# A squeeze-and-excitation gate on one core: 21-row chunks with finer read and write pieces, a shorter gate chain, and the weights on another queue

## Chip, cores, metric

The kernel runs on 1 core of one Trainium2 chip. The metric is the device time of one execution in microseconds (us). The kernel before takes 308.88 us, median of 5 runs (308.16 to 309.18). Single profiled executions have a "span", from first to last instruction, which is about 1.8 us shorter than the time of the run.

## The reference

```python
# x: (1, 256, 256, 384) bf16, w_down: (384, 24), w_up: (24, 384)
def reference(x, w_down, w_up):
    s = x.mean(axis=(1, 2))
    s = _sigmoid(_silu(s @ w_down) @ w_up)
    return x * s[:, None, None, :]
```

All of x must be read before the first output is known. x is 65,536 rows of 384 bf16 values, 50.33 MB. On the core it is laid out as 128 partitions with 512 rows each; below, "a row" is one such row on all 128 partitions, 98,304 bytes. The kernel before keeps 272 of the 512 rows on chip from the first reading to the write (17 slots of 16), so the other 240 are read a second time.

## The kernel before

It has two phases. In the read phase, chunks of 16 rows are loaded into 17 slots in rotation, and TensorE sums the rows by a matmul with ones. Then a short chain on several engines turns the sum into the gate `s_bc`. In the write phase, the 17 chunks still in the slots (272 rows) are multiplied by the gate on VectorE and written; each slot that has been written is filled again with one of the 15 chunks (240 rows) that were overwritten, which is then multiplied and written too.

```python
R = max(1, min(RPP, (16 * 1024) // (C * 2)))   # 21 ...
while R > 1 and RPP % R != 0: R -= 1           # ... cut down to 16, a divisor of 512
S_fit = max(1, (avail - 256) // slot_bytes)    # 17 slots
...
# the last chunk is read as 14 + 2 rows, every other one whole
# write pieces: slot 0 as 2,4,10 rows, slot 1 as 8,8, the others whole
...
# TensorE, per row:   ps_S[0:32, 0:384] += ones^T @ row
# gate chain:
for k in range(NK):                            # VectorE: three scalings into partitions 0, 32, 64
    v.tensor_scalar(out=mean3[32*k:32*k+1, 0:P], in0=ps_S[0:1, k*P:(k+1)*P], scalar1=inv_count, ...)
pe.matmul(ps_mT[:, 0:NK], mean3[0:65, 0:P], sel[0:65, 0:NK])   # transpose by a 65-row matmul
v.tensor_copy(meanT, ps_mT)                    # then w_down, silu, w_up, sigmoid -> s_bc
...
for it in items:                               # write phase, VectorE
    for (lo, hi) in it["pieces"]:
        v.tensor_tensor(slots[s][:, lo:hi, :], slots[s][:, lo:hi, :], s_bc..., ALU.mult)
        # the scalar queue then writes this piece; the sync queue refills the slot when all its pieces are out
```

Of the kernel before, what the change touches and what calls it, by code (L numbers as in the profile page):

```python
# [4 lines left out]



def bass_standalone__se_block__vision_kernel(
# [4 lines left out]
    out: bass.AP,  # L13
    rows_per_chunk=None,
    max_slots=None,
):
    dt = mybir.dt
    ACTF = mybir.ActivationFunctionType
    ALU = mybir.AluOpType
    bf16 = dt.bfloat16  # L20
    f32 = dt.float32

    P = nc.NUM_PARTITIONS
    B, H, W, C = x.shape
    Cw, RED = w_down.shape
# [4 lines left out]
    RPP = NROWS // P  # L30
    assert C % P == 0 and C <= 512
    NK = C // P
    assert NK <= 4
    assert RED <= P
    inv_count = 1.0 / float(NROWS)

    if rows_per_chunk is None:
        R = max(1, min(RPP, (16 * 1024) // (C * 2)))
        while R > 1 and RPP % R != 0:
            R -= 1  # L40
    else:
        R = max(1, min(int(rows_per_chunk), RPP))
    chunks = []
    rs = 0
    while rs < RPP:
        nr = min(R, RPP - rs)
        chunks.append((rs, nr))
        rs += nr
    NCH = len(chunks)

    xr = x.flatten_outer_dims().rearrange("(p n) c -> p n c", p=P)
# [4 lines left out]
    with contextlib.ExitStack() as es:  # L56
        E = es.enter_context

        ones = E(nc.sbuf_tensor("se_ones", [P, M1], bf16))
        s_bc = E(nc.sbuf_tensor("se_sbc", [P, C], bf16))  # L60
        mean3 = E(nc.sbuf_tensor("se_mean3", [P, P], bf16))
        sel = E(nc.sbuf_tensor("se_sel", [P, NK], bf16))
        meanT = E(nc.sbuf_tensor("se_meanT", [P, NK], bf16))
        wd_sb = E(nc.sbuf_tensor("se_wd", [P, NK, RED], bf16))
        wu_sb = E(nc.sbuf_tensor("se_wu", [P, C], bf16))
# [1 line left out]
        dT = E(nc.sbuf_tensor("se_dT", [P, P], bf16))  # L67

        ps_S = E(nc.psum_tensor("se_psS", [P, C], f32))
        ps_mT = E(nc.psum_tensor("se_psmT", [P, NK], f32))  # L70
        ps_d = E(nc.psum_tensor("se_psd", [P, 1], f32))
        ps_u = E(nc.psum_tensor("se_psu", [P, C], f32))

        slot_bytes = R * C * 2
        avail = nc.sbuf_bytes_remaining
        S_fit = max(1, (avail - 256) // slot_bytes)
        S = min(NCH, S_fit)
        if max_slots is not None:
            S = max(1, min(S, int(max_slots)))
        assert S >= 2 or NCH == 1  # L80
        slots = [E(nc.sbuf_tensor(f"se_slot{i}", [P, R, C], bf16)) for i in range(S)]

        sem_rd = [E(nc.semaphore(f"se_rd{i}")) for i in range(S)]
        sem_wr = [E(nc.semaphore(f"se_wr{i}")) for i in range(S)]
# [1 line left out]
        sem_dve = E(nc.semaphore("se_dve"))  # L86
        sem_w = E(nc.semaphore("se_w"))
        sem_ones = E(nc.semaphore("se_onesm"))
        sem_z = E(nc.semaphore("se_z"))
        sem_init = E(nc.semaphore("se_init"))  # L90
        sem_mean3 = E(nc.semaphore("se_m3"))
        sem_mT = E(nc.semaphore("se_mT"))
        sem_meanT = E(nc.semaphore("se_meanT"))
        sem_d = E(nc.semaphore("se_d"))
# [1 line left out]
        sem_dT = E(nc.semaphore("se_dTs"))  # L96
        sem_u = E(nc.semaphore("se_u"))
        sem_sbc = E(nc.semaphore("se_sbcs"))
        sem_tail = E(nc.semaphore("se_tail"))

        slot_of_chunk = [t % S for t in range(NCH)]
        NB = NCH - S
# [3 lines left out]
        for t in range(NCH):  # L106
            s = slot_of_chunk[t]
            fill_cnt[s] += 1
            phase1_fill_idx.append(fill_cnt[s])
        p1_pieces = []  # L110
        for t in range(NCH):
            rs_, nr = chunks[t]
            s = slot_of_chunk[t]
            if t == NCH - 1 and nr > 2:
                cut = nr - 2
                p1_pieces.append([(0, cut, sem_rd[s], 16 * phase1_fill_idx[t]), (cut, nr, sem_tail, 16)])
            else:
                p1_pieces.append([(0, nr, sem_rd[s], 16 * phase1_fill_idx[t])])

        items = []  # L120
        for s in range(S):
            c = resident_chunk_of_slot[s]
            nr = chunks[c][1]
            if s == 0:
                cuts = [0, min(2, nr), min(6, nr), nr]
            elif s == 1:
                cuts = [0, min(8, nr), nr]
            else:
                cuts = [0, nr]
            cuts = sorted(set(cuts))  # L130
            pieces = [(cuts[i], cuts[i + 1]) for i in range(len(cuts) - 1)]
            items.append(dict(chunk=c, slot=s, stream=False, pieces=pieces, fill_idx=phase1_fill_idx[c]))
        wr_cnt = [0] * S
        fill_cnt2 = list(fill_cnt)
# [12 lines left out]
        assert sorted(it["chunk"] for it in items) == list(range(NCH))  # L147

        with nc.Block() as block:
            @block.gpsimd  # L150
            def _(g):
                g.dma_start(wd_sb[:, :, :], w_down.rearrange("(k p) r -> p k r", p=P)).then_inc(sem_w, 16)  # L152
                g.dma_start(wu_sb[0:RED, :], w_up[:, :]).then_inc(sem_w, 16)  # L153

            @block.sync
            def _(sp):
                for t in range(NCH):
# [16 lines left out]
            @block.vector  # L174
            def _(v):
                v.memset(ones[:, :], 1.0).then_inc(sem_ones, 1)  # L176
                v.memset(mean3[:, :], 0.0).then_inc(sem_z, 1)  # L177
                v.memset(sel[:, :], 0.0).then_inc(sem_z, 1)
                v.wait_ge(sem_z, 2)
                for k in range(NK):  # L180
                    v.memset(sel[32 * k:32 * k + 1, k:k + 1], 1.0).then_inc(sem_init, 1)  # L181
                v.wait_ge(sem_pe, NCH)
                v.wait_ge(sem_z, 2)
                for k in range(NK):
                    v.tensor_scalar(  # L185
                        out=mean3[32 * k:32 * k + 1, 0:P],
                        in0=ps_S[0:1, k * P:(k + 1) * P],
                        scalar1=inv_count,
                        scalar2=None,
                        op0=ALU.mult,  # L190
                    ).then_inc(sem_mean3, 1)
                v.wait_ge(sem_mT, 1)
                v.tensor_copy(meanT[:, 0:NK], ps_mT[:, 0:NK]).then_inc(sem_meanT, 1)  # L193
                v.wait_ge(sem_sig, 1)
                v.wait_ge(sem_d, 1)
                v.tensor_tensor(  # L196
                    dT[0:RED, 0:P],
                    ps_d[0:RED, 0:1].broadcast_to([RED, P]),
                    sig[0:RED, 0:1].broadcast_to([RED, P]),
                    ALU.mult,  # L200
                ).then_inc(sem_dT, 1)
                v.wait_ge(sem_sbc, 1)
                for it in items:
                    s = it["slot"]
                    first = True
                    for (lo, hi) in it["pieces"]:
                        if first:
                            v.wait_ge(sem_rd[s], 16 * it["fill_idx"])
                            first = False
                        v.tensor_tensor(  # L210
                            slots[s][:, lo:hi, :],
                            slots[s][:, lo:hi, :],
                            s_bc[:, None, :].broadcast_to([P, hi - lo, C]),
                            ALU.mult,
                        ).then_inc(sem_dve, 1)

            @block.tensor
            def _(pe):
                pe.wait_ge(sem_ones, 1)
                n_mm_total = sum(nr for _, nr in chunks)  # L220
                mm_i = [0]

                def row_mms(s, lo, hi):
                    ins_ = None
                    for r in range(lo, hi):
                        ins_ = pe.matmul(  # L226
                            ps_S[0:M1, 0:C],
                            ones[:, 0:M1],
                            slots[s][:, r, :],
                            start=(mm_i[0] == 0),  # L230
                            stop=(mm_i[0] == n_mm_total - 1),
                        )
                        mm_i[0] += 1
                    return ins_

                for t in range(NCH):
                    s = slot_of_chunk[t]
                    ins = None
                    for (lo, hi, sm, wv) in p1_pieces[t]:
                        pe.wait_ge(sm, wv)  # L240
                        ins = row_mms(s, lo, hi)
                    ins.then_inc(sem_pe, 1)
                pe.wait_ge(sem_mean3, NK)
                pe.wait_ge(sem_init, NK)
                pe.matmul(ps_mT[:, 0:NK], mean3[0:32 * (NK - 1) + 1, 0:P], sel[0:32 * (NK - 1) + 1, 0:NK]).then_inc(sem_mT, 1)  # L245
                pe.wait_ge(sem_meanT, 1)
                pe.wait_ge(sem_w, 32)
                ins = None
                for k in range(NK):
                    ins = pe.matmul(  # L250
                        ps_d[0:RED, 0:1],
                        wd_sb[:, k, 0:RED],
                        meanT[:, k:k + 1],
                        start=(k == 0),
                        stop=(k == NK - 1),
                    )
                ins.then_inc(sem_d, 1)
                pe.wait_ge(sem_dT, 1)
                pe.matmul(ps_u[:, 0:C], dT[0:RED, 0:P], wu_sb[0:RED, 0:C]).then_inc(sem_u, 1)  # L259

            @block.scalar
            def _(act):
                act.wait_ge(sem_ones, 1)
                act.activation(sig[32:33, 0:1], ones[32:33, 0:1], ACTF.Sigmoid)  # L264
                act.wait_ge(sem_d, 1)
# [40 lines left out]
```

## Time and profile before

| reading | value |
|---|---|
| span of the profiled run | 306.7 us |
| last row matmul over, chain begins (chain of waits) | 125.4 us |
| `s_bc` ready | 128.5 us |
| from `s_bc` to the end | 178.2 us |
| a chunk of 16 rows in the read phase (timeline) | 3.69 us |

The page of the kernel before, first its slices (DMA is the mean busy share of the 16 DMA engines in tenths, GB/s what they moved in each fortieth of the span), then the bytes.

```profile
DMA  7999999999999997089999999999999999999998
GB/s 287 429 420 430 421 426 429 420 428 426 423 428 423 426 429 329 16 318 383 428 426 429 429 425 423 428 434 433 423 428 436 434 425 425 434 434 426 428 429 346
HBM read 73.96 MB, written 50.33 MB: 405 GB/s over the span
```

DMA is at work in nearly all slices, at 420 to 436 GB/s outside the start, the dent and the end. That the rate itself has little left is an estimate from these slices: none is above 436, and one at 428 is usual. So two ways to gain stand out: move fewer bytes, or shrink the dent in slices 16 to 19, where the read phase ends and the writes begin.

The timeline of the kernel before in that dent (columns: start us, duration us, engine, line, operation, output and inputs, count, and in brackets the idle time before it with its releaser).

```profile
119.30 2.77 PE L226 MATMUL se_psS<-se_slot,se_ones 128*32 128x384 bf16 x16 [0.91 <-DMA se_slot<-in_x_dram]
122.65 2.77 PE L226 MATMUL se_psS<-se_slot,se_ones 128*32 128x384 bf16 x16 [0.58 <-DMA se_slot<-in_x_dram]
125.47 0.90 DVE L185 TENSOR_SCALAR se_mean<-se_psS 1x128 bf16<-1x128 f32 x3 [124.12 <-PE se_psS L226]
...
128.02 0.49 ACT L268 ACTIVATE se_sbc<-se_psu 128x384 bf16<-128x384 f32 x1 [0.74 <-PE se_psu L259]
128.54 23.18 DVE L210 TENSOR_TENSOR se_slot<-se_slot,se_sbc 128x768 bf16<-128x768 bf16 x10 [0.95 <-ACT se_sbc L268]
```

TensorE starts the last chunk only at 122.65, when its 14-row piece has landed, and ends all 16 rows at 125.4. One row takes (2.77 - 0.33) / 15 = 0.163 us there (0.33 us is one matmul by itself, 335 ns on the page), against 0.23 us for its DMA (3.69 us for 16): TensorE is fast enough, it only gets the rows too late.

The same stretch in windows of 1 us (columns: window, its length, busy us and instructions of PE, PEld, DVE, ACT, POOL, granted TensorE clock, DMA share, GB/s).

```profile
120.00:121.00 1.00, 1.00 (x8) 0.61 (x7) 0.00 (x0) 0.00 (x0) 0.00 (x0) 1.00 0.79 295
121.00:122.00 1.00, 1.00 (x7) 0.42 (x5) 0.00 (x0) 0.00 (x0) 0.00 (x0) 1.00 0.23 94
122.00:123.00 1.00, 0.42 (x4) 0.22 (x4) 0.00 (x0) 0.00 (x0) 0.00 (x0) 1.00 0.12 45
123.00:124.00 1.00, 1.00 (x8) 0.61 (x7) 0.00 (x0) 0.00 (x0) 0.00 (x0) 1.00 0.00 0
...
130.00:131.00 1.00, 0.00 (x0) 0.00 (x0) 1.00 (x1) 0.00 (x0) 0.00 (x0) 0.91 0.73 267
131.00:132.00 1.00, 0.00 (x0) 0.00 (x0) 1.00 (x2) 0.00 (x0) 0.00 (x0) 0.50 0.82 323
132.00:133.00 1.00, 0.00 (x0) 0.00 (x0) 1.00 (x2) 0.00 (x0) 0.00 (x0) 0.50 0.22 92
```

Some DMA engines are done by 121 and a few trail (shares of 0.23 and 0.12) until 122.60. Then, by the packet records, nothing moves until 130.01, for 7.4 us. At 132 the writes have a hole again while VectorE (1.00 busy) works on the next piece.

### The profile page before, as it was taken

How to read it: one execution, taken by the hardware profiler on the slowest of the kernel's cores; microseconds unless marked ns; L12 is line 12 of the kernel's file. 1: busy time of each engine (PE TensorE's matmuls, PEld its weight loads, DVE VectorE, ACT ScalarE, POOL GpSimd, SP SyncE). 2: the span in 40 equal slices, each digit the busy share in tenths (PEclk: the TensorE clock that was granted, in tenths of full speed). 3: DMA queues.
4: the chain of work that ended last, by engine and by line, in shares of the span. 5: the costliest groups of instructions: out<-in, count | busy, mean ns of one | idle time of the engine just before them, and what ended most of it. 6: DMA issues, size and time to landing. Idle time of an engine off the chain costs nothing.

```text
span 306.7 us, 1211 instructions
## 1 busy us (share of the span) xinstructions
PE 92.7 (30%) x517; PEld 48.6 (16%) x517; DVE 107.1 (35%) x46; ACT 2.1 (1%) x4; POOL 1.7 (1%) x6
## 2 busy tenths in 40 slices
PE   0977787777777777400000000000000000000000
PEld 0544344444443333200000000000000000000000
DVE  0000000000000000499999999999444441000000
ACT  1000000000000000000000000000000000000000
POOL 2000000000000000000000000000000000000000
PEclk9999799999999999955555555555555555555555
DMA  7999999999999997089999999999999999999998
GB/s 287 429 420 430 421 426 429 420 428 426 423 428 423 426 429 329 16 318 383 428 426 429 429 425 423 428 434 433 423 428 436 434 425 425 434 434 426 428 429 346
DMA packets 12020, 124.36 MB, mean 405 GB/s; under 512 B 1364, under 2 KB 1648, under 8 KB 2160
## 3 DMA queue, kind: packets, MB, share of 16 engines
q1 hardware_dynamic: 6912, 73.93, 57.4%
q10 hardware_dynamic: 5040, 50.33, 38.9%
q8 instruction: 4, 0.07, 0.1%
q0 software_dynamic: 64, 0.04, 0.0%
HBM read 73.96 MB, written 50.33 MB: 405 GB/s over the span
## 4 chain that ended last, share of the span: by engine, by line
DMA 57%; DVE 14%; another core or an unknown queue 7%; PE 2%; SPq 2%; issue 0%; ACT 0%
DMA se_slot<-in_x_dram 42%; DMA out_dram<-se_slot 15%; DVE se_slot L210 14%; PE se_psS L226 2%; SPq L163 1%; SPq L170 0%; DVE se_mean L185 0%; ACT se_sbc L268 0%; PE se_psu L259 0%; DVE se_dT L196 0%; PE se_psd L250 0%; PE se_psmT L245 0%; DVE se_meanT L193 0%; ACT se_sig L266 0%
## 5 line engine op out<-in xcount | busy, mean ns | idle before, releaser
L210 DVE TENSOR_TENSOR se_slot<-se_slot,se_sbc 128x6144 bf16<-128x6144 bf16 (+4 forms) x35 | 105.4, 3080 | 21.2 <-DMA se_slot<-in_x_dram 20.2
L226 PE MATMUL se_psS<-se_slot,se_ones 128*32 128x384 bf16 x512 | 91.9, 335 | 33.5 <-DMA se_slot<-in_x_dram 33.5
L226 PEld LDWEIGHTS se_psS<-se_slot,se_ones 128*32 128x32 bf16 x512 | 48.3, 99 | 76.7 <-DMA se_slot<-in_x_dram 37.3
L185 DVE TENSOR_SCALAR se_mean<-se_psS 1x128 bf16<-1x128 f32 x3 | 0.8, 280 | 124.2 <-PE se_psS L226 124.1
L264 ACT ACT_TABLE_LOAD x1 | 1.3, 1283 | 0.7 <-PEq L291 0.7
L266 ACT ACTIVATE se_sig<-se_psd 24x1 f32<-24x1 f32 x1 | 0.2, 160 | 124.9 <-PE se_psd L250 124.9
L152 POOL DMA_DIRECT2D se_wd<-in_w_down_dram x1 | 0.9, 923 | 0.8 <-POOLq L291 0.8
L153 POOL DMA_DIRECT2D se_wu<-in_w_up_dram x1 | 0.5, 542 | 0.0
L259 PE MATMUL se_psu<-se_wu,se_dT 24*128 24x384 bf16 x1 | 0.3, 331 | 0.6 <-DVE se_dT L196 0.6
L268 ACT ACTIVATE se_sbc<-se_psu 128x384 bf16<-128x384 f32 x1 | 0.5, 490 | 0.7 <-PE se_psu L259 0.7
L245 PE MATMUL se_psmT<-se_sel,se_mean 65*128 65x3 bf16 x1 | 0.2, 177 | 1.0 <-DVE se_mean L185 1.0
L196 DVE TENSOR_TENSOR se_dT<-se_psd,se_sig 24x128 bf16<-24x128 f32 x1 | 0.3, 279 | 0.5 <-ACT se_sig L266 0.5
L176 DVE MEMSET se_ones<- 128x32 bf16 x1 | 0.1, 85 | 0.8 <-PEq L291 0.8
L245 PEld LDWEIGHTS se_psmT<-se_sel,se_mean 65*128 65x128 bf16 x1 | 0.1, 95 | 1.4 <-DVE se_mean L185 1.4
L250 PE MATMUL se_psd<-se_meanT,se_wd 128*24 128x1 bf16 x3 | 0.2, 166 | 0.3 <-DVE se_meanT L193 0.3
L193 DVE CAST se_meanT<-se_psmT 128x3 bf16<-128x3 f32 x1 | 0.2, 162 | 0.3 <-PE se_psmT L245 0.3
L181 DVE MEMSET se_sel<- 1x1 bf16 x3 | 0.2, 59 | 0.2
L264 ACT ACTIVATE se_sig<-se_ones 1x1 f32<-1x1 bf16 x1 | 0.2, 202 | 0.0
L259 PEld LDWEIGHTS se_psu<-se_wu,se_dT 24*128 24x128 bf16 x1 | 0.1, 90 | 0.7 <-DVE se_dT L196 0.7
L250 PEld LDWEIGHTS se_psd<-se_meanT,se_wd 128*24 128x24 bf16 x3 | 0.1, 90 | 0.3 <-DVE se_meanT L193 0.3
L177 DVE MEMSET se_mean<- 128x64 uint32 x1 | 0.1, 112 | 0.0
L291 POOL MEMSET const-bfloat16-1.0<- 128x1 bf16 x1 | 0.1, 102 | 0.0
(4 smaller groups left out, 0.4 us busy)
## 6 DMA issues: line engine op xcount, KB each, us to landing
se_slot<-in_x_dram SPq DMA_DIRECT2D x46, 1536.0 KB, 31.7
out_dram<-se_slot ACTq DMA_DIRECT2D x30, 1536.0 KB, 41.2
out_dram<-se_slot ACTq DMA_DIRECT2D x2, 768.0 KB, 6.3
se_slot<-in_x_dram SPq DMA_DIRECT2D x1, 1344.0 KB, 39.2
out_dram<-se_slot ACTq DMA_DIRECT2D x1, 960.0 KB, 3.7
out_dram<-se_slot ACTq DMA_DIRECT2D x1, 384.0 KB, 2.3
se_slot<-in_x_dram SPq DMA_DIRECT2D x1, 192.0 KB, 36.4
out_dram<-se_slot ACTq DMA_DIRECT2D x1, 192.0 KB, 1.9
```

Of the source, the lines that this page charges most:

```text
L152: g.dma_start(wd_sb[:, :, :], w_down.rearrange("(k p) r -> p k r", p=P)).then_inc(sem_w, 16)
L153: g.dma_start(wu_sb[0:RED, :], w_up[:, :]).then_inc(sem_w, 16)
L163: sp.dma_start(slots[s][:, lo:hi, :], xr[:, rs_ + lo:rs_ + hi, :]).then_inc(sm, 16)
L185: v.tensor_scalar(out=mean3[32 * k:32 * k + 1, 0:P], in0=ps_S[0:1, k * P:(k + 1) * P], scalar1=inv_count, scalar2=None, op0=ALU.mult,).the ...
L196: v.tensor_tensor(dT[0:RED, 0:P], ps_d[0:RED, 0:1].broadcast_to([RED, P]), sig[0:RED, 0:1].broadcast_to([RED, P]), ALU.mult,).then_inc(sem ...
L210: v.tensor_tensor(slots[s][:, lo:hi, :], slots[s][:, lo:hi, :], s_bc[:, None, :].broadcast_to([P, hi - lo, C]), ALU.mult,).then_inc(sem_dv ...
L226: ins_ = pe.matmul(ps_S[0:M1, 0:C], ones[:, 0:M1], slots[s][:, r, :], start=(mm_i[0] == 0), stop=(mm_i[0] == n_mm_total - 1),)
L245: pe.matmul(ps_mT[:, 0:NK], mean3[0:32 * (NK - 1) + 1, 0:P], sel[0:32 * (NK - 1) + 1, 0:NK]).then_inc(sem_mT, 1)
L250: ins = pe.matmul(ps_d[0:RED, 0:1], wd_sb[:, k, 0:RED], meanT[:, k:k + 1], start=(k == 0), stop=(k == NK - 1),)
L259: pe.matmul(ps_u[:, 0:C], dT[0:RED, 0:P], wu_sb[0:RED, 0:C]).then_inc(sem_u, 1)
L264: act.activation(sig[32:33, 0:1], ones[32:33, 0:1], ACTF.Sigmoid)
L268: act.activation(s_bc[:, 0:C], ps_u[:, 0:C], ACTF.Sigmoid).then_inc(sem_sbc, 1)
```

## The change

It means to keep the same traffic and shorten the dent: larger chunks (a slot of 21 rows), the rest of 8 rows as the first chunk, finer read pieces at the end, finer write pieces at the start, a gate chain with one scaling, and the weight loads on the scalar queue instead of gpsimd. (It also adds a function that plans read pieces; nothing calls it.) The core of the diff:

```diff
-        R = max(1, min(RPP, (16 * 1024) // (C * 2)))
-        while R > 1 and RPP % R != 0:
-            R -= 1
+        R = max(1, min(RPP, 21))
...
+    rem0 = RPP % R
+    if rem0:
+        chunks.append((0, rem0))          # 8 rows, first
...
-        S_fit = max(1, (avail - 256) // slot_bytes)
+        S_fit = max(1, (avail - 64) // slot_bytes)
...
+        tails = {NCH - 3: [9, 12], NCH - 2: [12, 9], NCH - 1: [6, 5, 4, 3, 2, 1]}
...                                        # each further piece has its own semaphore
             if s == 0:
-                cuts = [0, min(2, nr), min(6, nr), nr]
+                pieces = make_pieces(nr, list(first_item_pieces))     # 2,3,3,4,4,5
             elif s == 1:
-                cuts = [0, min(8, nr), nr]
+                pieces = make_pieces(nr, [5, 5, 5, 6])
+            elif s == 2:
+                pieces = make_pieces(nr, [7, 7, 7])
...
-                for k in range(NK):
-                    v.tensor_scalar(out=mean3[32 * k:32 * k + 1, 0:P], in0=ps_S[0:1, k * P:(k + 1) * P], ...)
+                v.tensor_scalar(out=meanr[0:1, 0:C], in0=ps_S[0:1, 0:C], ...)
...
-                pe.matmul(ps_mT[:, 0:NK], mean3[0:32 * (NK - 1) + 1, 0:P], sel[...])
+                for k in range(NK):
+                    ins = pe.matmul(ps_mT[:, k * 512:k * 512 + 1], meanr[0:1, k * P:(k + 1) * P], ones[0:1, 0:1], start=True, stop=True)
...
-                g.dma_start(wd_sb..., w_down...); g.dma_start(wu_sb..., w_up...)       # gpsimd
+                act.dma_start(wd_sb..., w_down...); act.dma_start(wu_sb..., w_up...)   # scalar
```

More of the change, by code (lines that the diff above doesn't have):

```diff
@@ L4, with _phase1_read_pieces @@
 from concourse import mybir
+def _phase1_read_pieces(chunks, pe_rate_frac=0.24, min_piece=2, extra=2):
+    pieces_per_chunk = {}
+    rem = 0
+    plan = []
+    for t in reversed(range(len(chunks))):
+        nr = chunks[t][1]
+        cuts_rev = []
+        left = nr
+        while left > 0:
+            cap = max(min_piece, int(pe_rate_frac * rem) + extra)
+            sz = min(left, cap)
+            cuts_rev.append(sz)
+            rem += sz
+            left -= sz
+        sizes = list(reversed(cuts_rev))
+        lo = 0
+        pl = []
+        for sz in sizes:
+            pl.append((lo, lo + sz))
+            lo += sz
+        pieces_per_chunk[t] = pl
+        if len(pl) == 1 and sizes[0] == nr and rem - nr >= 4 * nr:
+            break
+    for t in range(len(chunks)):
+        if t in pieces_per_chunk:
+            plan.append(pieces_per_chunk[t])
+        else:
+            plan.append([(0, chunks[t][1])])
+    return plan
 def bass_standalone__se_block__vision_kernel(
@@ L15, in bass_standalone__se_block__vision_kernel @@
     max_slots=None,
+    use_scratch=False,
+    first_item_pieces=(2, 3, 3, 4, 4, 5),
 ):
@@ L32, in bass_standalone__se_block__vision_kernel @@
     NK = C // P
-    assert NK <= 4
     assert RED <= P
@@ L43, in bass_standalone__se_block__vision_kernel @@
     chunks = []
+    rem0 = RPP % R
     rs = 0
+    if rem0:
+        chunks.append((0, rem0))
+        rs = rem0
     while rs < RPP:
-        nr = min(R, RPP - rs)
-        chunks.append((rs, nr))
-        rs += nr
+        chunks.append((rs, R))
+        rs += R
     NCH = len(chunks)
@@ L60, in bass_standalone__se_block__vision_kernel @@
         s_bc = E(nc.sbuf_tensor("se_sbc", [P, C], bf16))
-        mean3 = E(nc.sbuf_tensor("se_mean3", [P, P], bf16))
-        sel = E(nc.sbuf_tensor("se_sel", [P, NK], bf16))
+        meanr = E(nc.sbuf_tensor("se_meanr", [P, C], bf16))
         meanT = E(nc.sbuf_tensor("se_meanT", [P, NK], bf16))
@@ L69, in bass_standalone__se_block__vision_kernel @@
         ps_S = E(nc.psum_tensor("se_psS", [P, C], f32))
-        ps_mT = E(nc.psum_tensor("se_psmT", [P, NK], f32))
+        ps_mT = E(nc.psum_tensor("se_psmT", [P, NK * 512], f32))
         ps_d = E(nc.psum_tensor("se_psd", [P, 1], f32))
@@ L75, in bass_standalone__se_block__vision_kernel @@
         avail = nc.sbuf_bytes_remaining
-        S_fit = max(1, (avail - 256) // slot_bytes)
-        S = min(NCH, S_fit)
+        S_fit = max(1, (avail - 64) // slot_bytes)
+        slots = []
+        if use_scratch and nc.dynamic_dma_scratch_size is not None and nc.dynamic_dma_scratch_size >= slot_bytes:
+            slots.append(nc.alloc_sbuf_tensor_at("se_slot_scr", [P, R, C], bf16, offset=0))
+        S = S_fit + len(slots)
+        S = min(NCH, S)
         if max_slots is not None:
@@ L80, in bass_standalone__se_block__vision_kernel @@
         assert S >= 2 or NCH == 1
-        slots = [E(nc.sbuf_tensor(f"se_slot{i}", [P, R, C], bf16)) for i in range(S)]
+        while len(slots) < S:
+            slots.append(E(nc.sbuf_tensor(f"se_slot{len(slots)}", [P, R, C], bf16)))
+        slots = slots[:S]
         sem_rd = [E(nc.semaphore(f"se_rd{i}")) for i in range(S)]
@@ L88, in bass_standalone__se_block__vision_kernel @@
         sem_ones = E(nc.semaphore("se_onesm"))
-        sem_z = E(nc.semaphore("se_z"))
-        sem_init = E(nc.semaphore("se_init"))
-        sem_mean3 = E(nc.semaphore("se_m3"))
+        sem_mean = E(nc.semaphore("se_mean"))
         sem_mT = E(nc.semaphore("se_mT"))
@@ L98, in bass_standalone__se_block__vision_kernel @@
         sem_sbc = E(nc.semaphore("se_sbcs"))
-        sem_tail = E(nc.semaphore("se_tail"))
         slot_of_chunk = [t % S for t in range(NCH)]
@@ L109, in bass_standalone__se_block__vision_kernel, with make_pieces @@
             phase1_fill_idx.append(fill_cnt[s])
+        tails = {NCH - 3: [9, 12], NCH - 2: [12, 9], NCH - 1: [6, 5, 4, 3, 2, 1]}
+        piece_plan = []
+        for t in range(NCH):
+            z = tails.get(t, [chunks[t][1]])
+            piece_plan.append([(sum(z[:i]), sum(z[:i + 1])) for i in range(len(z))])
         p1_pieces = []
+        extra_piece_sems = 0
         for t in range(NCH):
-            rs_, nr = chunks[t]
             s = slot_of_chunk[t]
-            if t == NCH - 1 and nr > 2:
-                cut = nr - 2
-                p1_pieces.append([(0, cut, sem_rd[s], 16 * phase1_fill_idx[t]), (cut, nr, sem_tail, 16)])
-            else:
-                p1_pieces.append([(0, nr, sem_rd[s], 16 * phase1_fill_idx[t])])
+            pl = []
+            for i, (lo, hi) in enumerate(piece_plan[t]):
+                if i == 0:
+                    pl.append((lo, hi, sem_rd[s], 16 * phase1_fill_idx[t]))
+                else:
+                    sm = E(nc.semaphore(f"se_p1x{extra_piece_sems}"))
+                    extra_piece_sems += 1
+                    pl.append((lo, hi, sm, 16))
+            p1_pieces.append(pl)
+        assert extra_piece_sems <= 16
+        def make_pieces(nr, sizes):
+            cuts = [0]
+            for z in sizes:
+                cuts.append(min(nr, cuts[-1] + z))
+            if cuts[-1] < nr:
+                cuts.append(nr)
+            cuts = sorted(set(cuts))
+            return [(cuts[i], cuts[i + 1]) for i in range(len(cuts) - 1)]
         items = []
@@ L124, in bass_standalone__se_block__vision_kernel @@
             if s == 0:
-                cuts = [0, min(2, nr), min(6, nr), nr]
+                pieces = make_pieces(nr, list(first_item_pieces))
             elif s == 1:
-                cuts = [0, min(8, nr), nr]
-            else:
-                cuts = [0, nr]
-            cuts = sorted(set(cuts))
-            pieces = [(cuts[i], cuts[i + 1]) for i in range(len(cuts) - 1)]
+                pieces = make_pieces(nr, [5, 5, 5, 6])
+            elif s == 2:
+                pieces = make_pieces(nr, [7, 7, 7])
+            else:
+                pieces = [(0, nr)]
             items.append(dict(chunk=c, slot=s, stream=False, pieces=pieces, fill_idx=phase1_fill_idx[c]))
@@ L149, in bass_standalone__se_block__vision_kernel @@
         with nc.Block() as block:
-            @block.gpsimd
-            def _(g):
-                g.dma_start(wd_sb[:, :, :], w_down.rearrange("(k p) r -> p k r", p=P)).then_inc(sem_w, 16)
-                g.dma_start(wu_sb[0:RED, :], w_up[:, :]).then_inc(sem_w, 16)
             @block.sync
@@ L176, in _ @@
                 v.memset(ones[:, :], 1.0).then_inc(sem_ones, 1)
-                v.memset(mean3[:, :], 0.0).then_inc(sem_z, 1)
-                v.memset(sel[:, :], 0.0).then_inc(sem_z, 1)
-                v.wait_ge(sem_z, 2)
-                for k in range(NK):
-                    v.memset(sel[32 * k:32 * k + 1, k:k + 1], 1.0).then_inc(sem_init, 1)
-                v.wait_ge(sem_pe, NCH)
-                v.wait_ge(sem_z, 2)
-                for k in range(NK):
-                    v.tensor_scalar(
-                        out=mean3[32 * k:32 * k + 1, 0:P],
-                        in0=ps_S[0:1, k * P:(k + 1) * P],
-                        scalar1=inv_count,
-                        scalar2=None,
-                        op0=ALU.mult,
-                    ).then_inc(sem_mean3, 1)
+                v.wait_ge(sem_pe, NCH)
+                v.tensor_scalar(
+                    out=meanr[0:1, 0:C],
+                    in0=ps_S[0:1, 0:C],
+                    scalar1=inv_count,
+                    scalar2=None,
+                    op0=ALU.mult,
+                ).then_inc(sem_mean, 1)
                 v.wait_ge(sem_mT, 1)
-                v.tensor_copy(meanT[:, 0:NK], ps_mT[:, 0:NK]).then_inc(sem_meanT, 1)
+                v.tensor_copy(meanT[:, 0:NK], ps_mT[:, 0:NK * 512:512]).then_inc(sem_meanT, 1)
                 v.wait_ge(sem_sig, 1)
@@ L242, in _ @@
                     ins.then_inc(sem_pe, 1)
-                pe.wait_ge(sem_mean3, NK)
-                pe.wait_ge(sem_init, NK)
-                pe.matmul(ps_mT[:, 0:NK], mean3[0:32 * (NK - 1) + 1, 0:P], sel[0:32 * (NK - 1) + 1, 0:NK]).then_inc(sem_mT, 1)
+                pe.wait_ge(sem_mean, 1)
+                ins = None
+                for k in range(NK):
+                    ins = pe.matmul(
+                        ps_mT[:, k * 512:k * 512 + 1],
+                        meanr[0:1, k * P:(k + 1) * P],
+                        ones[0:1, 0:1],
+                        start=True,
+                        stop=True,
+                    )
+                ins.then_inc(sem_mT, 1)
                 pe.wait_ge(sem_meanT, 1)
@@ L262, in _ @@
             def _(act):
+                act.dma_start(wd_sb[:, :, :], w_down.rearrange("(k p) r -> p k r", p=P)).then_inc(sem_w, 16)
+                act.dma_start(wu_sb[0:RED, :], w_up[:, :]).then_inc(sem_w, 16)
                 act.wait_ge(sem_ones, 1)
```

## The prediction

> **What bounds the kernel now.** Traffic. The page counts 73.96 MB read and 50.33 MB written; the slices show 420 to 436 GB/s nearly everywhere. The timeline shows a 16-row chunk every 3.69 us in the read phase (426 GB/s), and 7.32 us per read-and-write pair later (430 GB/s). [...] 124.3 MB at 428 GB/s is 290 us of the 306.7 us span. The rest is start, end and the gap between the phases: in 1 us windows the DMA share falls to 0.23 and 0.12 from 121 to 123 us (a few engines finish late), is zero from 123 to 130, with holes at 132, 137 and 142-144 us worth 2.4 us.
>
> The gap by the timeline: the last bytes land at about 123.0; TensorE starts the 14-row piece only at 122.65 and ends all 16 rows at 125.44 (0.163 us a row); the gate chain (three 0.28 us scalings, transpose 0.18, copy 0.16, matmuls, sigmoids) gives s_bc at 128.54; the first two rows are multiplied by 129.1.
>
> **What the change does to traffic: almost nothing.** [...] 13 slots of 21 rows (16,128 bytes each) fit: 273 resident rows against 17 x 16 = 272. Re-read: 239 rows against 240, worth 0.23 us. With 12 slots it would be 20 rows more, +4.7 us.
>
> **Terms (estimates from trace durations):**
> - End of the read phase: pieces of 6,5,4,3,2,1 rows let TensorE keep up (0.163 us a row against 0.23 us for DMA). It ends about 123.4 instead of 125.44. -2.0 us, all critical.
> - Chain: one 384-wide scaling of about 0.55 us replaces three (0.90 us with gaps); three 1-row matmuls replace one, +0.05. -0.3 us.
> - Larger packets: 12,288-byte packets take 460 ns, 1,536-byte ones 65 ns, so about 8 ns is fixed; at 16,128 bytes the rate rises about 0.4%, -1.1 us over the run. Small pieces cost about 77 ns each: +0.8. Net -0.3.
> - First writes: pieces 2,3,3,4,4,5 / 5,5,5,6 / 7,7,7 instead of 2,4,10 / 8,8. DVE multiplies a row in 0.20 us plus 0.16 us a piece, DMA writes one in 0.23, so DVE is hardly ahead. Finer pieces remove the 4-to-10-row hole; their fixed costs and the jump to 21 rows (4.35 us) give some back, but by then re-reads fill the queues. Net -0.6 us.
> - Weights on the scalar queue, fewer memsets, 8-row chunk 0: off the path, 0.
>
> Sum -3.2 us, about 1%. Nearly all gains lie in 121 to 145 us.
>
> **Prediction: 305.6 us, 8 in 10 between 303.4 and 307.6.** Chances: faster by over 2% 0.09, within 2% 0.88, slower by over 2% 0.03.
>
> **What would show each step.** MB read and written unchanged (within 0.2 MB). TensorE's last row under 0.8 us after the last landing; the chain from there to s_bc about 2.8 us; zero-DMA stretch shrinks from 7 to about 5 us. Packet count falls; full-stream rate 427 to 432 GB/s. Fewer holes in the 10 us after the first write, with perhaps one before the first 21-row piece.
>
> **What would make it wrong.** 12 slots. TensorE idling longer between 21-row chunks and falling to half clock (as after 2.2 us idle at 34 us: 0.32 us a matmul): at the tail it would lag by 1 to 2 us. Larger packets helping more, or late engines trailing by more.

(Two passages are cut: one on how fast DMA can get, one on how much memory is left for slots; no run of this case shows either. That the rate has little left was the author's estimate. That 13 slots fit was shown by the result, 73.86 MB read. No term of the sum is cut: -2.0 - 0.3 - 0.3 - 0.6 - 0 = -3.2 us.)

## The result and the profile after

The changed kernel takes 304.2 us (median of 8 runs, 303.96 to 304.66); the kernel before took 308.88 us over 15 runs of that measurement. The ratio is 0.9857 (95% interval 0.9843 to 0.987), 1.4% faster. A ratio here is the mean time of one kernel's fast runs over that of the other's fast runs of the same rounds, so it is not quite the ratio of the medians quoted.

The page of the changed kernel, the same lines as before.

```profile
DMA  7999999999999999199999999999999999999998
GB/s 284 439 424 424 431 422 442 410 442 416 439 420 429 420 423 389 58 376 399 411 422 435 437 418 439 435 422 437 427 433 437 422 435 435 422 437 427 433 437 343
HBM read 73.86 MB, written 50.33 MB: 411 GB/s over the span
```

The bytes are the same but for one row (0.10 MB). The dent is smaller: 389, 58, 376, 399 where it was 329, 16, 318, 383.

The timeline of the changed kernel in the dent.

```profile
115.74 7.57 PE L268 MATMUL se_psS<-se_slot,se_ones 128*32 128x384 bf16 x42 [0.67 <-DMA se_slot<-in_x_dram]
122.16 0.27 PEld L268 LDWEIGHTS se_psS<-se_slot,se_ones 128*32 128x32 bf16 x3 [0.24 <-DMA se_slot<-in_x_dram]
122.65 0.32 PEld L268 LDWEIGHTS se_psS<-se_slot,se_ones 128*32 128x32 bf16 x3 [0.22 <-DMA se_slot<-in_x_dram]
123.35 0.55 DVE L227 TENSOR_SCALAR se_meanr<-se_psS 1x384 bf16<-1x384 f32 x1 [122.46 <-PE se_psS L268]
123.95 0.22 PE L288 MATMUL se_psmT<-se_ones,se_meanr 1*128 1x1 bf16 x3 [0.64 <-DVE se_meanr L227]
...
125.59 0.49 ACT L320 ACTIVATE se_sbc<-se_psu 128x384 bf16<-128x384 f32 x1 [0.74 <-PE se_psu L309]
126.11 26.40 DVE L252 TENSOR_TENSOR se_slot<-se_slot,se_sbc 128x768 bf16<-128x768 bf16 x16 [0.95 <-ACT se_sbc L320]
```

TensorE now follows the pieces: when it takes up the last two at 122.65 (they landed at 122.60 and 122.84 by the trace's semaphore events), only 3 rows are left, and the scaling starts at 123.35 instead of 125.47. The chain from there to `s_bc` takes 2.74 us instead of 3.05.

The same windows of 1 us in the changed kernel.

```profile
121.00:122.00 1.00, 1.00 (x8) 0.40 (x5) 0.00 (x0) 0.00 (x0) 0.00 (x0) 1.00 0.26 94
122.00:123.00 1.00, 1.00 (x8) 0.41 (x6) 0.00 (x0) 0.00 (x0) 0.00 (x0) 1.00 0.06 21
123.00:124.00 1.00, 0.36 (x4) 0.05 (x3) 0.55 (x1) 0.00 (x0) 0.00 (x0) 1.00 0.00 0
...
127.00:128.00 1.00, 0.00 (x0) 0.00 (x0) 1.00 (x3) 0.00 (x0) 0.00 (x0) 0.50 0.42 152
128.00:129.00 1.00, 0.00 (x0) 0.00 (x0) 1.00 (x3) 0.00 (x0) 0.00 (x0) 0.50 0.89 333
129.00:130.00 1.00, 0.00 (x0) 0.00 (x0) 1.00 (x2) 0.00 (x0) 0.00 (x0) 0.50 1.04 391
```

The few trailing engines are still there (0.26), at the same time. By the packet records the stretch without any DMA lasts from 122.34 to 127.58, 5.2 us instead of 7.4. (Windows that are wholly empty number 4 instead of 7, which makes the gain look larger than it is.) After the first write there is no hole like the one at 132.

By phase, `s_bc` is ready 2.43 us earlier (126.09 against 128.52), and the write phase is 1.77 us shorter (176.41 against 178.18): 4.2 us of span. In the first 40 us after `s_bc` the changed kernel moved 15.71 MB against 15.29 (from the GB/s of windows), and 0.42 MB at 430 GB/s is 1.0 us. The other 0.8 us is one row less and a slightly faster stream. That shows in the VectorE timeline, where late in the streaming each multiplication waits for a read, so their starts give the period of one chunk read and one chunk written. The kernel before, 16 rows:

```profile
236.22 3.36 DVE L210 TENSOR_TENSOR se_slot<-se_slot,se_sbc 128x6144 bf16<-128x6144 bf16 x1 [3.96 <-DMA se_slot<-in_x_dram]
243.54 3.36 DVE L210 TENSOR_TENSOR se_slot<-se_slot,se_sbc 128x6144 bf16<-128x6144 bf16 x1 [3.96 <-DMA se_slot<-in_x_dram]
```

And the changed kernel, 21 rows:

```profile
221.75 4.36 DVE L252 TENSOR_TENSOR se_slot<-se_slot,se_sbc 128x8064 bf16<-128x8064 bf16 x1 [5.20 <-DMA se_slot<-in_x_dram]
231.33 4.36 DVE L252 TENSOR_TENSOR se_slot<-se_slot,se_sbc 128x8064 bf16<-128x8064 bf16 x1 [5.22 <-DMA se_slot<-in_x_dram]
```

Over all such rows the period is 7.316 us per 32 rows (0.2286 a row) before and 9.567 us per 42 rows (0.2278) after. Over 751 rows (239 re-read and 512 written) that is 0.6 us.

### The profile page after: what moved, and what is told of

Same layout as the page of the kernel before. It is cut to its first block, busy times and chain, and to the rows that moved or that the text cites. A ratio compares the mean times of both kernels' runs of the same rounds, so it can differ in the third digit from the quotient of the medians.

```text
span 302.5 us, 1200 instructions
## 1 busy us (share of the span) xinstructions
PE 93.0 (31%) x519; PEld 49.2 (16%) x519; DVE 106.4 (35%) x39; ACT 2.1 (1%) x4; POOL 0.2 (0%) x4
## 3 DMA queue, kind: packets, MB, share of 16 engines
HBM read 73.86 MB, written 50.33 MB: 411 GB/s over the span
## 4 chain that ended last, share of the span: by engine, by line
DMA 51%; DVE 16%; another core or an unknown queue 6%; SPq 6%; PE 4%; issue 0%; ACT 0%
DMA se_slot<-in_x_dram 36%; DVE se_slot L252 16%; DMA out_dram<-se_slot 15%; SPq L212 6%; PE se_psS L268 4%; SPq L219 0%; DVE se_meanr L227 0%; ACT se_sbc L320 0%; PE se_psu L309 0%; DVE se_dT L238 0%; PE se_psd L300 0%; PE se_psmT L288 0%; DVE se_meanT L235 0%; ACT se_sig L318 0%
## 5 line engine op out<-in xcount | busy, mean ns | idle before, releaser
L252 DVE TENSOR_TENSOR se_slot<-se_slot,se_sbc 128x8064 bf16<-128x8064 bf16 (+7 forms) x35 | 105.4, 3078 | 22.5 <-DMA se_slot<-in_x_dram 21.5
```

## The experiments

The theory was that of the prediction: the gain lies in the dent, from TensorE's lag and the starved first writes, plus a small one from larger packets. The rivals were that small pieces cost as much as they save, that re-reads fill the holes anyway, and that larger chunks are a gain of their own. Every run below was correct; times are medians of its runs. The columns "`s_bc`" and "after it" split the span of the profiled run, read from the chain of waits.

| run | time us | ratio to before | `s_bc` at | after it |
|---|---|---|---|---|
| before | 308.88 | 1 | 128.52 | 178.18 |
| changed | 304.2 | 0.9857 | 126.09 | 176.41 |
| again (control) | 304.2 | 0.9857 | 126.04 | 176.36 |
| u_tail | 306.46 | 0.993 | 128.30 | 176.40 |
| t_last_only | 305.67 | 0.9898 | 127.59 | 176.41 |
| u_first | 306.18 | 0.9919 | 126.06 | 178.44 |
| u_chain | 304.43 | 0.9865 | 126.18 | 176.42 |
| u_weights | 304.35 | 0.9856 | 126.20 | 176.40 |
| u_chunk16 | 305.61 | 0.9894 | 126.58 | 177.82 |
| u_cuts_chunk16 (5 fast runs of 6) | 306.85 | 0.9936 | profile slow | profile slow |
| u_cuts_chunk16_b | 306.56 | 0.9947 | 126.38 | 178.02 |
| b_chunk21_restfirst | 309.04 | 1.0013 | 128.84 | 178.26 |
| b_chunk21_restlast | 311.72 | 1.0098 | 128.41 | 181.39 |
| slots14 | 299.5 | 0.9699 | 125.98 | 171.52 |

Only `u_tail`, `u_first` and `u_chain` ran with the control. The others ran on other chips, each with the kernel before beside it but without the changed kernel. "Slower" below is the difference of medians from 304.2 us; the ratios give a second reading: 1.3 us instead of 1.47 for `t_last_only`, 1.1 instead of 1.41 for `u_chunk16`, none instead of 0.15 for `u_weights`, and a gain of 4.9 instead of 4.7 for `slots14`. The 95% interval of a single ratio is about 0.4 to 0.6 us to either side.

The control came out as the changed kernel had: 304.18 to 304.24 in 4 runs.

> The changed kernel itself, unedited, as the control of this call: 304.2 us, 4.6 us under the kernel before. All the runs of this call are compared with it.

**The read tail undone.**

```diff
-        tails = {NCH - 3: [9, 12], NCH - 2: [12, 9], NCH - 1: [6, 5, 4, 3, 2, 1]}
+        tails = {NCH - 1: [19, 2]}
```

> The changed kernel with the last read chunk cut 19+2 and the two before it whole. Theory (TensorE's lag after the last byte is what the pieces remove): TensorE then starts 19 rows only when they have landed and ends 21 rows later at 0.163 us a row, about 125.5 us instead of 123.3, so +1.8 to +2.4 us against the changed kernel (306.0 to 306.6). Rival (the nine extra DMAs cost 77 ns each and eat a good part of it): +1.0 to +1.4 us. Phase 2 the same to 0.2 us under both.

It is 2.26 us slower, as the theory said, and all of it lies before `s_bc`. The timeline of this run:

```profile
121.94 3.59 PE L268 MATMUL se_psS<-se_slot,se_ones 128*32 128x384 bf16 x21 [0.81 <-DMA se_slot<-in_x_dram]
125.56 0.55 DVE L227 TENSOR_SCALAR se_meanr<-se_psS 1x384 bf16<-1x384 f32 x1 [124.67 <-PE se_psS L268]
```

TensorE idles 0.81 us for the 19 rows and then needs 3.59 us for all 21. (The edit takes away six DMAs, 10 pieces against 4, not the nine that the expectation counts; with six the rival would have said some 0.2 us more, still well under 2.26.)

**Only the last chunk in pieces.**

```diff
-        tails = {NCH - 3: [9, 12], NCH - 2: [12, 9], NCH - 1: [6, 5, 4, 3, 2, 1]}
+        tails = {NCH - 1: [6, 5, 4, 3, 2, 1]}
```

> The changed kernel with only the last read chunk in pieces; the two before it whole. Theory (TensorE at 0.163 us a row against 0.23 us of DMA must have started early enough to have no backlog): the whole second-last chunk is done only about 1.2 us before the last landing, 21 rows are then left, TensorE ends some 2.2 us after the last landing instead of 0.8: +1.2 to +1.5 us. Rival (only the last chunk's small pieces matter): within 0.2 us, or 0.2 faster for the DMAs saved.

It is 1.47 us slower than the changed kernel (1.3 by the ratios). The timeline of this run:

```profile
117.82 7.00 PE L268 MATMUL se_psS<-se_slot,se_ones 128*32 128x384 bf16 x42 [1.23 <-DMA se_slot<-in_x_dram]
124.86 0.55 DVE L227 TENSOR_SCALAR se_meanr<-se_psS 1x384 bf16<-1x384 f32 x1 [123.96 <-PE se_psS L268]
```

TensorE starts the whole second-last chunk at 117.82 and then works without a pause through 42 rows; the small pieces land before it gets to them. So of the 2.26 us, the cuts of the chunks ahead of the last are worth 1.3 to 1.5 and the six small pieces alone only 0.8 to 1.0. The backlog has to be prevented a chunk earlier.

**The first write cuts undone** (carried over to 21 rows).

```diff
-    first_item_pieces=(2, 3, 3, 4, 4, 5),
+    first_item_pieces=(2, 4, 15),
...
-                pieces = make_pieces(nr, [5, 5, 5, 6])
+                pieces = make_pieces(nr, [8, 13])
...
-                pieces = make_pieces(nr, [7, 7, 7])
+                pieces = make_pieces(nr, [21])
```

> The changed kernel with the first writes cut 2,4,15 / 8,13 / 21 (the old cuts carried over to 21 rows). Theory (VectorE hardly ahead, coarse pieces starve the DMA right after the gate): +0.9 to +1.8 us against the changed kernel, seen as fewer bytes moved in the first 10 us after s_bc and nowhere else. Rival (re-reads fill whatever the writes leave, so the cuts hardly matter): under 0.3 us.

It is 1.98 us slower, and 2.03 us of span lie after `s_bc`. Windows of 2 us of this run, the second and third after `s_bc` (DMA share and GB/s are the last two columns):

```profile
128.06:130.06 2.00, 0.00 (x0) 0.00 (x0) 2.00 (x1) 0.00 (x0) 0.00 (x0) 0.50 0.53 206
130.06:132.06 2.00, 0.00 (x0) 0.00 (x0) 2.00 (x2) 0.00 (x0) 0.00 (x0) 0.50 0.44 184
```

And of the changed kernel:

```profile
128.09:130.09 2.00, 0.00 (x0) 0.00 (x0) 2.00 (x3) 0.00 (x0) 0.00 (x0) 0.50 0.97 368
130.09:132.09 2.00, 0.00 (x0) 0.00 (x0) 2.00 (x3) 0.00 (x0) 0.00 (x0) 0.50 1.02 402
```

VectorE is fully busy in both. With a 15-row piece (about 3.2 us by 0.20 us a row and 0.16 a piece, from the 3.36 us of 16 rows and 4.36 of 21) its write can start only when the whole piece is done. The loss comes back nowhere.

**The gate chain undone** (the old chain, as in the kernel before).

```diff
-                v.tensor_scalar(out=meanr[0:1, 0:C], in0=ps_S[0:1, 0:C], ...)
+                for k in range(NK):
+                    v.tensor_scalar(out=mean3[32 * k:32 * k + 1, 0:P], in0=ps_S[0:1, k * P:(k + 1) * P], ...)
...
+                pe.matmul(ps_mT[:, 0:NK], mean3[0:65, 0:P], sel[0:65, 0:NK])    # instead of three 1-row matmuls
```

> The changed kernel with the old gate chain (three scalings into three partitions, one 65-row transposing matmul). Theory: +0.30 to +0.35 us, all between the last row matmul and s_bc (3.08 us instead of 2.75). Rival: the new chain's three single-row matmuls [...] eat the gain: under 0.1 us.

The chain is 3.05 us again instead of 2.74, the expected 0.31. In the profiled run the last row came 0.2 us earlier, so that `s_bc` was only 0.09 us later; by the medians of all runs the time rose by 0.23 us.

**The weights on gpsimd again.**

```diff
+            @block.gpsimd
+            def _(g):
+                g.dma_start(wd_sb[:, :, :], w_down...).then_inc(sem_w, 16)
+                g.dma_start(wu_sb[0:RED, :], w_up[:, :]).then_inc(sem_w, 16)
...
-                act.dma_start(wd_sb..., w_down...); act.dma_start(wu_sb..., w_up...)
```

> The changed kernel with the two weight loads back on the gpsimd queue. Theory: off the path, within 0.2 us of the changed kernel. Rival: the software queue delays the first chunk or the end of the program, +0.3 us or more.

It is 0.15 us slower by the medians and no slower by the ratios (0.9856 against 0.9857), and the changed kernel itself ranged from 303.96 to 304.66 us. So no effect is shown: off the path, as expected. But see the last experiment.

**16-row chunks.**

```diff
-        R = max(1, min(RPP, 21))
+        R = max(1, min(RPP, 16))
...
+        tails = {NCH - 3: [7, 9], NCH - 2: [9, 7], NCH - 1: [5, 4, 3, 2, 1, 1]}
+    first_item_pieces=(2, 3, 3, 4, 4),    # then 5,5,6 and 8,8
```

> The changed kernel with 16-row chunks (17 slots, 272 resident rows, 240 re-read), pieces scaled to 16 rows. Theory (the fixed 8 ns of every packet and one re-read row): +0.7 us in the read phase, +0.5 us in the rest, +0.2 us for the row, together +1.2 to +1.5 us; streaming period per row back to 0.2286 us from 0.2277. Rival (packet size is nothing, the gain lies all in the gap): under 0.4 us.

It is 1.41 us slower, within the theory's range (1.1 by the ratios, just under it): 0.49 us before `s_bc` and 1.41 after it in the profiled run (which was the slowest of its 4 runs, 306.2 us). By an estimate from the packets these account for most of it: in the traces' records of each DMA packet, one of 768 bytes takes 36 ns (changed kernel), of 1,536 bytes 65 (both kernels), of 12,288 bytes (a 16-row chunk, kernel before) 460, of 16,128 bytes (21 rows, changed kernel) 601. Between the first and the last the slope is 27.2 bytes per ns, times 16 engines 435 GB/s, with 7.8 ns fixed per packet. So 21 rows cost 0.45% less per byte than 16, an estimated 1.3 us over some 290 us of transfers. The run also had to change the read and write pieces, so it does not separate the packets from these.

**16-row chunks and the old write cuts at once** (2,4,10 / 8,8 / 16).

> The changed kernel with 16-row chunks and the old write cuts (2,4,10 / 8,8 / 16) at once; the new read tail and gate chain stay. Theory (the cuts are worth 2 us only because the next whole piece is 21 rows, 4.35 us of VectorE; with 16-row chunks, 3.35 us, they are worth little): the phase after s_bc is that of the kernel before, 178.2 us, so about 306.0 us, +0.4 us against the changed kernel with 16-row chunks (305.6). Rival (the two parts add up): +2.0 us on it, 307.6 us.

Its five fast runs gave 306.08 to 307.29 us, ratio 0.9936; the profiled one was slow (see the end) and can't be split. So it ran a second time:

> The same kernel once more, because the profile of the run before fell in a slow state [...] and can't be split into phases. Expected, from its fast runs: 306.1 to 307.3 us, and the phase after s_bc 178.0 to 178.9 us, against 177.8 with 16-row chunks and the new cuts and 178.2 in the kernel before. If the cuts and the chunk size simply added up, it would be 179.8.

This time it took 305.88 to 307.34 us, and the phase after `s_bc` took 178.02 us in the profiled run, not 179.8. Against `u_chunk16` the old cuts cost 1.0 to 1.2 us by the medians and about 1.3 to 1.6 us by the ratios, between the theory (0.4) and the rival (2.0); but in the two profiled runs the phase after `s_bc` differs by only 0.20 us (177.82 and 178.02). So the cuts are worth less with 16-row chunks than with 21, and whether they are worth more than I said stays open. The 16-row kernels scatter by 0.9 to 1.5 us from run to run where the 21-row ones stay within 0.7 (mostly under 0.4), and what the scatter comes from I did not find.

**The kernel before with 21-row chunks alone.**

```diff
-        R = max(1, min(RPP, (16 * 1024) // (C * 2)))
-        while R > 1 and RPP % R != 0:
-            R -= 1
+        R = max(1, min(RPP, 21))
...
+    rs = RPP % R
+    if rs:
+        chunks.append((0, rs))
```

> The kernel before with nothing but 21-row chunks, the rest of 8 rows first (the write cuts become 2,4,15 / 8,13 / 21). Theory (the packets gain 1.2 to 1.4 us, the coarse pieces lose as much): within 0.5 us of the kernel before, the phase after s_bc 178.4 us as where only the cuts were undone. Rival (larger chunks are a gain of their own): -1.2 to -1.6 us.

No gain: ratio 1.0013 (0.9997 to 1.0029). The rival falls. TensorE's lag at the end grows by 5 rows at 0.163 us, 0.8 us, but the scaling starts only 0.32 us later (125.79 instead of 125.47), so the read phase before it gains an estimated 0.5 us, and the phase after `s_bc` stays at 178.26 us. That its coarser pieces lose there what the packets gain fits `u_first`, where the same cuts cost 2.03 us after `s_bc`.

**The same with the rest of 8 rows last.**

```diff
     while rs < RPP:
         nr = min(R, RPP - rs)
         chunks.append((rs, nr))      # the old loop: 24 chunks of 21, then 8
```

> The same, but with the rest of 8 rows as the last chunk, as the old chunk loop would leave it. A resident slot then holds 8 rows instead of 21: 260 resident, 252 re-read, 1.28 MB more read. Theory (a re-read row costs 0.2277 us): +3.0 us against the rest-first run. Rival (order of the chunks does not matter): the same to 0.3 us.

It reads 75.14 MB instead of 73.86 and is 2.68 us slower than the rest-first run; after `s_bc` it is 3.13 us, the 13 rows at 0.23 us or so, and 0.43 us come back because the last chunk to be summed is short. A small detail of the change, where the rest stands, decides as much as any other part.

**14 slots: a version that beats both.** One argument of the build is set to 256. The kernel takes as many slots as fit in the bytes that remain, and with this argument that is 14 instead of 13: 16,128 bytes more on each partition. The run has no DMA on the gpsimd queue. That nothing in it needs these bytes was the author's estimate; the run was correct.

```diff
-    nc = _bacc.Bacc("TRN2", target_bir_lowering=False, num_devices=1)
+    nc = _bacc.Bacc("TRN2", target_bir_lowering=False, num_devices=1, dynamic_dma_scratch_size=256)
```

> The changed kernel [...]: 14 slots, 294 resident rows, 218 re-read instead of 239. Theory (traffic at 0.2277 us a row is the bound): -4.8 us, about 299.4 us, 2.06 MB less read. Rival (the drain or the gap swallow it): under 3 us.

The page of this run:

```profile
q1 hardware_dynamic: 6192, 71.76, 57.4%
q10 hardware_dynamic: 5476, 50.37, 40.1%
q8 instruction: 4, 0.07, 0.1%
HBM read 71.80 MB, written 50.33 MB: 411 GB/s over the span
```

It takes 299.5 us, 3.0% less than the kernel before and 4.7 us less than the changed one: 21 rows fewer to re-read, at 0.228 us each, 4.8. Nearly all of it (4.9 us of span) lies after `s_bc`. This one argument is worth as much as the whole change. The page of the kernel before lists a further queue, `q0 software_dynamic` with 64 packets, for the weights on gpsimd; the pages of the changed kernel and of this run do not. Whether the same argument works with the weights on gpsimd was not run.

## Why the prediction was right

The prediction said 305.6 us, within 2%, and 303.4 to 307.6; it was 304.2.

- **Traffic unchanged, 13 slots:** right; 73.86 MB against 73.96 read, which is 239 rows read twice instead of 240.
- **End of the read phase, -2.0 us:** right; undoing it costs 2.26. TensorE had 3 rows left at 122.65 and was done at 123.3, as said (123.4), and the stretch without DMA shrank to 5.2 us (said: about 5). The fear that longer pauses would bring half clock at the tail did not come true: the granted clock reads 1.00 in every window from 112 to 126 us.
- **Chain, -0.3 us:** right; 0.31 in the chain. The one wide scaling took 0.55 us, as said.
- **Weights, memsets, 8-row chunk off the path:** right; no effect of the weights is shown. But the place of the 8-row chunk is worth 2.68 us against the obvious alternative, which the prediction counted correctly without saying that it was a choice.
- **Packets, "Net -0.3":** mis-sized; this is the first step that failed. The gross term was right (1.1 us, plus 0.23 for the row, which I worked out and then left out of the sum; together 1.1 to 1.4 measured, with the pieces changed too). The charge of 0.8 us for small pieces was most likely wrong as an added term: the read pieces lie in the dent, where the term for the end of the read phase counts their cost in net. No run measures the charge alone, but without six of the read pieces (`u_tail`) the reads end some 0.46 us earlier (the chain of waits has the landing at 121.89; the last packet of the changed kernel ends at 122.34; one profile each, 76 ns a piece), and the run is 2.26 us slower all the same. The packet records give an estimate close to it: 128 packets on 16 engines are 8 on each, at 7.8 ns fixed, and one of 4 bytes that takes 9 ns, 71 ns a piece. So the 77 ns a piece may well be right; they are already inside the 2.26.
- **First writes, "Net -0.6 us":** mis-sized. On the prediction's own terms, the new cuts at 21 rows against the old ones at 16, the windows after `s_bc` give 1.0 us. It also depends on the chunk: undone at 21 rows it is 1.98 us, at 16 rows 0.2 to 1.6. The prediction counted the jump to 21 rows only as something that gives a little back; part of the job of the cuts is to repair what 21-row chunks break.

The two together made the sum 1.2 to 1.5 us too small. By phase nearly all of the miss lies after `s_bc`: up to there the change brought 2.43 us, and the prediction had 2.3 for the tail and the chain; after it the change brought 1.77, and the prediction had 0.6 for the cuts and some part of 0.3 for the packets. The single undone parts add up to 2.26 + 1.98 + 0.23 + 0.15 + 1.41 = 6.0 us (5.5 by the ratios), more than the 4.4 (1 - 0.9857 of 308.6) that the change brought, since the parts depend on each other: `b_chunk21_restfirst` shows that larger chunks without the cuts are worth nothing.

## What to carry to other kernels

When a kernel runs at its DMA rate, count the bytes first: one more resident slot (4.7 us) was worth as much as all the careful repairs of a dent, and the place of a remainder chunk was worth 2.7 us. Where a reduction follows a stream, cut the stream early enough that the reducing engine has no backlog when the small last pieces come; cutting only the last chunk gave 0.8 to 1.0 of 2.26 us. Larger chunks and finer pieces at the ends belong together: undo one part at a time and also do it alone, because the worth of a part depends on the others.

## What else the traces show

- Over the packets of both kernels, from 768 to 16,128 bytes, the median times of reads and writes of x fit 7.8 ns plus bytes at 27.2 GB/s per engine within some 3%. Going from 12,288 to 16,128 bytes still gave 0.45% in packet time (460 and 601 ns).
- In the kernel before TensorE stood idle from 32.1 to 34.35 us, 2.22 us, and from 35.24 to 38.65 us the granted clock was 0.50, as windows of 1 us show (the clock is the third column from the end).

```profile
33.00:34.00 1.00, 0.00 (x0) 0.00 (x0) 0.00 (x0) 0.00 (x0) 0.00 (x0) 1.00 0.96 406
36.00:37.00 1.00, 1.00 (x4) 0.45 (x3) 0.00 (x0) 0.00 (x0) 0.00 (x0) 0.50 1.11 467
39.00:40.00 1.00, 1.00 (x8) 0.61 (x7) 0.00 (x0) 0.00 (x0) 0.00 (x0) 1.00 0.96 406
```

  In the changed kernel the same followed a pause of 2.66 us that ended at 30.86: clock 0.50 from 30.96 to 34.37 us. After that, up to 126.5 us, the clock stayed at 1.00, with pauses of 1.22 to 1.29 us between most 21-row chunks. The page of `u_chunk16` shows no such fall at all (second line; the first is the kernel before; tenths of the full clock in 40 slices, the 7 is the fall). Whether the pauses cause the falls is not shown.

```profile
PEclk9999799999999999955555555555555555555555
PEclk9999999999999999955555555555555555555555
```

- In one of all the runs (the first of `u_cuts_chunk16`, 369.9 us) matmuls took about 0.35 us a row in the whole read phase, for some 180 us, against 0.163 elsewhere. The page of that run shows TensorE busy through about twenty slices and DMA stopped before the sum was done. The views give a clock of 1.00 for all of it, which does not show that the clock was full: they also give 1.00 in the kernel before from 8 to 11 us, where its trace has no clock record yet (the first begins at 11.35 us) and its matmuls start 0.32 us apart. The cause stays open.

```profile
PE   2999999999999999999930000000000000000000
DMA  8999999999999200000019999999999999999997
```
